# Top-k attention with a channel mix on one core: scaling the mix's differences on GpSimd, and one slot more between ranks and mask

## The chip, the core and the metric

The kernel runs on one core of a Trainium2 chip. Its engines are TensorE (PE in the rows; PEld its weight loads), VectorE (DVE), ScalarE (ACT), GpSimd (POOL) and SyncE (SP), which issues the DMAs. Each engine works through its own queue in order, and they wait for one another by semaphores. The metric is the time of one execution on the device in microseconds; lower is better.

## What is computed

Attention over 8 batches, 8 heads, 576 positions and head size 64, in which every query keeps its 32 largest scores alone, and behind it a channel mix with a shift by one token (512 channels, 1024 inside):

```python
scores = scale * np.matmul(q, k.transpose(0, 1, 3, 2))
kth = np.partition(scores, -top_k, axis=-1)[..., -top_k:-top_k + 1]
scores = np.where(scores >= kth, scores, -1e9)
attn = softmax(scores)                       # over the kept ones
x = (attn @ v) laid out as (B, S, H * D)
x_prev = x shifted by one token
xk = mu_k * x + (1.0 - mu_k) * x_prev        # xr the same with mu_r
k = np.maximum(xk @ w_k, 0.0)
out = sigmoid(xr @ w_r) * (k * k @ w_v)
```

All tensors are float32. Where a matrix product of the mix needs more precision than one pass has, values are split into a coarse and a remaining part and three products are summed.

## The kernel before

**Tiles.** A tile of attention is 128 rows by 576 keys: 128 queries of one head, or the last 64 queries of two heads. A pair of heads has nine tiles, a batch 36, all of it 288. The mix goes over 19 chunks of tokens, most of 256 (`SIZES`).

**Slots.** The function `pipeline` writes the order of work out by hand, under a manual schedule. Each turn of its main loop is a slot, in which every engine gets one step of each of several tiles: tile n begins, and the older tiles n-1, n-2 and so on (`A`, `C`, `M`, `V`, `W`) are at later steps. The string `ORDER` gives the order of the steps in a slot; as each engine takes its instructions in the order in which they are issued, `ORDER` sets the order in each queue. A tile goes through these slots:

- slot n: TensorE makes the scores (lines 192 and 197, PSUM tile `ps`), ScalarE copies them to `sc` (`keep`, line 202).
- slot n+1: VectorE takes the eight best of each of seven pieces of a row (`c0` to `c6`, line 226): 56 candidates.
- slot n+2: VectorE ranks the candidates, three rounds of eight (lines 229 and 232), and writes the two bounds into `seen` (lines 237 and 238). ScalarE then takes the sign of every score against the 24th best, and a sum of it (`count`, line 242, tile `sg`). GpSimd multiplies it by the scores (`below`, line 245), which leaves the scores beneath the bound to be told from the others.
- slot n+3: ScalarE writes the exponentials to PSUM (`exp`, line 253, tile `se`; the tile is n-`EXPS`). VectorE takes the eight best of the product (`eighth`, line 819), picks the threshold by the count (`thr`, line 250), and masks the exponentials (`mask`, line 256, tile `E`).
- slot n+4: TensorE turns the masked tile (line 269), ScalarE copies it out (line 273); for the last tile of a group, VectorE takes the reciprocals of the row sums (line 283) and GpSimd spreads them (line 288, tile `rb`).
- slot n+5: TensorE turns these (line 294) and weighs the values (line 321). Slot n+6: VectorE scales the outcome into `xT` (`place`, lines 327 and 329).

**The mix** is handed to the slots in pieces by a planner, the class `Lanes`. Pieces of TensorE work (lines 377 to 379) go into the step `mix`, at most four a slot, as far as a budget reaches. Work of ScalarE and GpSimd waits in a queue for each of them (`L.soft`), with a planned cost, and is issued in the step `act` or `pool`, near the end of the slot, once what it depends on has been issued and the engine's budget for the slot allows. The function `begin` prepares a chunk twice, for the gate and for the hidden layer, in two halves of the channels: `change` takes the differences of neighbouring tokens (GpSimd, line 348), `share` multiplies them by 1 - mu, one scale per partition (ScalarE, line 353), and `add` adds the token (GpSimd, line 358). `finish` splits the sum into coarse (ScalarE, line 372) and remaining part (GpSimd, line 373). Behind the hidden layer GpSimd also works on its squares (lines 397 and 398). At the start the weights are prepared in the same slots (lines 121 to 158). When the tokens of a chunk aren't there yet, the mix waits (`"later"`).

Of the kernel before, what the change touches and what calls it, by code (L numbers as in the profile page):

```python
# [9 lines left out]
F32 = mybir.dt.float32  # L10
# [3 lines left out]
AF = mybir.ActivationFunctionType  # L14
OP = mybir.AluOpType
PSUM = bass.MemoryType.PSUM

B, H, S, D = 8, 8, 576, 64
# [18 lines left out]
NEG = -3.0e38  # L37
PACE, TENSOR, SHARE, PIECE, CAP, MOST = 4.60, 3.90, 0.74, 0.71, 4.45, 4
END, HASTE = 36, 0.56
EXPS, EVAC = 3, (0, 'et')  # L40
ORDER = """exp wpool high wmul norm evac best0 c0 drop0 c1 best1 c2 drop1 first score turn inv loads keep sign c3 best2 c4 bounds eighth norm2 count et late below act c5 early thr c6 mask place mix weigh wpe dve pool weights""".split()


@with_exitstack
def topk_attention_channel_mix(ctx: ExitStack, tc: tile.TileContext, q, k, v, mu_k, mu_r, w_k, w_v, w_r, out):
    nc = tc.nc
# [17 lines left out]
    nmu = consts.tile([128, 2, HP], F32, name="nmu")  # L64
# [8 lines left out]
    def open_pools(stack, g, sfx):  # L73
        p = lambda n, bufs, **kw: stack.enter_context(tc.tile_pool(name=n + sfx, bufs=bufs, **kw))
        g.one = p("one", 1)
        g.two = p("two", 2)
        g.three = p("three", 3)
        g.four = p("four", 4)


        scored = p("psS", 1, space=PSUM).tile([128, 2, 512], F32, name="ps")
        g.ps = scored[:, :, :HS]
        g.sums = scored[:, :, HS:HS + 128], scored[:, 0, HS + 128:HS + 192]

        se = p("psE", 1, space=PSUM).tile([128, 2 * 512], F32, name="se")
        g.pe, g.ranks = se[:, :S], se[:, S:S + 9]
        nc.vector.tensor_copy(g.ranks, ranks_i)
        g.ready = range(3 * HP + NFB) if sfx else []
        g.psM = p("psM", 4, space=PSUM)
# [108 lines left out]
        return g.ps  # L198

    def keep(g, T):  # L200
        T.sc = g.four.tile([128, S], F32, name="sc")
        nc.scalar.activation(T.sc.rearrange("p (e k) -> p e k", e=2), T.ps, AF.Copy)  # L202

    def pick_exact(g, T):
        top = g.four.tile([128, TOPK], F32, name="top")
# [34 lines left out]
    def count(g, T):  # L240
        T.side = g.two.tile([128, S], F32, name="sg")
        nc.scalar.activation(T.side, T.sc, AF.Sign, bias=T.under, scale=-BELOW, accum_out=T.cnt)  # L242

    def below(T):
        nc.gpsimd.tensor_mul(T.side, T.sc, T.side)  # L245
# [87 lines left out]
    def begin(g, pieces, which, n, L):  # L333

        halves = [Env() for _ in range(2)]
        for i, X in enumerate(halves):
            parts = []
            for h in (0, 1):
                o = 0
                for xT, s, m in pieces:  # L340
                    parts.append((h, o, xT, s, m))
                    o += m

            def change(X=X, parts=parts, h0=2 * i):
                if which:
                    g.change[h0 // 2] = g.one.tile([128, 2, CH], F32, name=f"xd{h0}")
                for _, o, xT, s, m in parts[:len(pieces)]:
                    nc.gpsimd.tensor_sub(g.change[h0 // 2][:, :, o:o + m], xT[:, h0:h0 + 2, s:s + m], xT[:, h0:h0 + 2, s + 1:s + 1 + m])

            def share(X=X, h0=2 * i):  # L350
                X.xm = g.two.tile([128, 2, CH], F32, name="xm")
                for h in (0, 1):
                    nc.scalar.activation(X.xm[:, h, :n], g.change[h0 // 2][:, h, :n], AF.Copy, scale=nmu[:, which, h0 + h:h0 + h + 1])

            def add(X=X, parts=parts, h0=2 * i):
                for _, o, xT, s, m in parts[:len(pieces)]:
                    d = X.xm[:, :, o:o + m]
                    nc.gpsimd.tensor_add(d, d, xT[:, h0:h0 + 2, s + 1:s + 1 + m])

            l = g.shared[i]  # L360
            if which:
                l = [L.soft("pool", 0.0046 * n + 0.05 * len(pieces), change, *l)]
            g.shared[i] = [L.soft("act", 0.0021 * n + 0.12, share, *l)]
            X.mixed = L.soft("pool", 0.0046 * n + 0.05 * len(pieces), add, *g.shared[i])
        return halves

# [235 lines left out]
    def pipeline(g):  # L602
        L = Lanes()
# [17 lines left out]
        xT, tiles, state = {}, {}, {"tokens": 0, "wait": 0, "start": 0, "held": []}  # L621
# [75 lines left out]
        def coming(n):  # L697

            for p in range(1, len(visits)):
                t = n - starts[p]  # L700
                if -5 <= t <= 5:
                    yield Ps[p] if p in Ps else new_pair(p), t

        total = len(where)
# [2 lines left out]
        load_mu()  # L707
        units = {}
        n = 0
        while n < total + 7 or "next" in state or L.busy():  # L710
            p, i = where[n] if n < total else (None, None)
            A, C, M, V, W = (tiles.get(n - d) for d in (1, 2, 3, 4, 5))
            X = tiles.get(n - EXPS)
            last = W if W and ends(W) else None

            def loads():
                for N, t in coming(n):
                    early = N.n > 1
                    if N.own and t == (-5 if early else -4):
                        load_keys(g, N, N.batch, N.hp)  # L720
                    if t == (-4 if early else -3):
                        load_queries(g, N, N.batch, N.hp, N.c0, N.c1)
                    if t == 5:
                        load_v(g, N, N.batch, N.hp)
                L.run("dma")

# [66 lines left out]
                    bounds(g, C)  # L793

            def count_():
                if C:
                    count(g, C)
                    L.use("act", 0.76)

            def below_():  # L800
                if C:
                    below(C)
                    L.use("pool", 1.36)

            def keep_():
# [22 lines left out]
                    L.use("dve", 3.4)  # L828

            def place_():  # L830
                T = tiles.get(n - 6)
                if T and ends(T):
                    U = T.U
                    if U.P.b not in xT:
                        if state["start"] < (U.P.b - 1) * S:
                            save()
                        if U.P.b > 1:
                            L.force(g.read)
                        xT[U.P.b] = new_batch(g, U.P.b)
                    U.xT = xT[U.P.b]  # L840
                    place(U)
                    if U.P.last and T.i == U.P.part[-1]:
                        state["tokens"] = U.P.b * S + (S if T.i == 8 else 256)
                if V and V.i == V.P.part[-1] and V.P.last:
                    o = slice(V.P.first, V.i + 1)
                    nc.vector.tensor_reduce(least[:, V.P.n // HP:V.P.n // HP + 1], V.P.group[:, :, 1:, o], axis=mybir.AxisListType.XYZ, op=OP.min)

            do = dict(loads=loads, score=score, turn=turn_, inv=inv, exp=exp, weigh=weigh_, norm=norm, norm2=norm2, bounds=bounds_,
                      count=count_, below=below_, keep=keep_, mix=mix, eighth=eighth, thr=thr, mask=mask_, place=place_, weights=weights)
# [12 lines left out]
    with ExitStack() as stack:  # L862
        g = Env()
# [15 lines left out]
    with tc.If(again > 0):  # L879
        with tc.For_i(0, B, 1) as b, ExitStack() as stack:  # L880
            g = Env()
            open_pools(stack, g, "_again")
            L = Direct()
            xT = new_batch(g)
            rows = out[bass.ds(b, 1)].rearrange("o s d -> (o s) d")
            for hp in range(HP):
# [3 lines left out]
                for i in range(9):  # L890
                    T = Tile_()
# [52 lines left out]
```

## Time and profile before

| | |
|---|---|
| time, median of 3 runs | 1282.28 us (1280.83 to 1283.04) |
| the profiled execution's own time | 1280.38 us |
| its span, first to last instruction | 1278.5 us |
| TensorE busy | 1149.8 us |
| VectorE busy | 1107.6 us |
| ScalarE busy | 1043.6 us |
| GpSimd busy | 903.1 us |
| mean granted share of TensorE's clock | 0.952 |

The span is what the trace covers; the execution's own time has 1.9 us more around it, and it lies 1.9 us below the median of the runs. Busy times of groups of instructions can sum to more than their engine's, since neighbouring instructions overlap a little. The name in front of an arrow in a row is the tile that is written, those behind it are read; L245 is line 245 of the kernel before.

### The profile page before, as it was taken

The page shows a single profiled execution, that of the slowest core. Times are in us where ns is not written, and L with a number is a line of the kernel's source. Part 1 is how long each engine was busy: PE and PEld are TensorE (multiplying, and loading weights), DVE is VectorE, ACT ScalarE, POOL GpSimd, SP SyncE. Part 2 cuts the span into 40 slices and gives each one's busy share as a digit, 9 for nine tenths or more (in the row PEclk, how much of TensorE's full clock was granted, in tenths as well). Part 3 has the DMA queues.
Part 4 walks back from the last instruction along what each step waited for, and adds up shares of the span by engine and source line. Part 5 has one row for each costly group of instructions (what it writes and reads, how often), then busy time and mean ns, then how long its engine had stood idle before and what let it go on. Part 6 is the DMA issues. An engine that isn't in the chain of part 4 may idle for free.

```text
span 1278.5 us, 33370 instructions
## 1 busy us (share of the span) xinstructions
PE 1149.8 (90%) x10757; PEld 893.0 (70%) x10757; DVE 1107.6 (87%) x6368; ACT 1043.6 (82%) x2494; POOL 903.1 (71%) x829
## 2 busy tenths in 40 slices
PE   5767798996989898889989999999999998999997
PEld 2435586774868686676867677877787786778886
DVE  5999999999989899899999999999999998998000
ACT  4786988988888888798989889989899988898431
POOL 5998765757676766586668777778677857777652
PEclk8787899998989899799999999999999998999999
DMA  5332122112111122112211122122211221111000
GB/s 160 122 108 79 31 59 62 34 41 65 50 51 50 29 73 62 36 28 64 64 55 41 29 72 63 40 57 52 65 51 39 65 64 44 51 30 28 13 17 24
DMA packets 113768, 69.37 MB, mean 54 GB/s; under 512 B 81840, under 2 KB 106416, under 8 KB 113584
## 3 DMA queue, kind: packets, MB, share of 16 engines
q1 hardware_dynamic: 113584, 67.14, 19.1%
q8 instruction: 88, 1.44, 0.5%
q14 instruction: 96, 0.79, 0.2%
HBM read 57.68 MB, written 9.44 MB: 52 GB/s over the span
## 4 chain that ended last, share of the span: by engine, by line
PE 49%; DVE 22%; ACT 14%; POOL 11%; issue 2%; SPq 1%; DMA 0%; ACTq 0%; DVEq 0%; POOLq 0%
PE ps L321 10%; PE ps L192 7%; DVE cand L226 5%; DVE top L819 4%; POOL sg L245 4%; DVE E L256 4%; ACT sc L202 4%; PE pv L377 4%; PE pv L379 3%; PE pt L269 3%; PE ph L377 3%; PE pv L378 3%; PE ph L378 3%; PE ph L379 3%; ACT sg L242 3%; PE pz L377 2%
## 5 line engine op out<-in xcount | busy, mean ns | idle before, releaser
L245 POOL TENSOR_TENSOR sg<-sc,sg 128x576 f32<-128x576 f32 x288 | 409.5, 1422 | 251.9 <-ACT sg L242 251.2
L226 DVE MAX8 cand<-sc 128x8 f32<-128x82 f32 (+1 forms) x2016 | 466.8, 232 | 1.6 <-ACT sc L202 1.4
L202 ACT ACTIVATE sc<-ps 128x576 f32<-128x576 f32 x288 | 188.8, 656 | 120.7 <-PE ps L192 54.7
L819 DVE MAX8 top<-sg 128x8 f32<-128x576 f32 x288 | 217.2, 754 | 31.2 <-POOL sg L245 29.1
L242 ACT ACTIVATE sg<-sc,seen 128x576 f32<-128x576 f32 x288 | 224.3, 779 | 18.9 <-DVE seen L237 16.1
L256 DVE SCALAR_TENSOR_TENSOR E<-sc,seen,se 128x576 f32<-128x576 f32 x288 | 231.8, 805 | 0.8 <-DVE cand L226 0.6
L192 PE MATMUL ps<-K,qs 64*128 64x288 f32 x1024 | 202.6, 472 | 32.7 <-ACT sc L202 16.2
L253 ACT ACTIVATE se<-sc,seen 128x576 f32<-128x576 f32 x288 | 218.8, 760 | 12.0 <-DVE E L256 10.7
L273 ACT ACTIVATE et<-pt 128x320 f32<-128x320 f32 x576 | 219.4, 440 | 1.5 <-PE pt L269 0.8
L321 PE MATMUL ps<-et,v_in 128*64 128x128 f32 (+1 forms) x2560 | 177.0, 286 | 44.1 <-ACT sc L202 39.6
L321 PEld LDWEIGHTS ps<-et,v_in 128*64 128x64 f32 x2560 | 146.7, 149 | 69.7 <-ACT sc L202 56.1
L269 PEld LDWEIGHTS pt<-ident,E 64*128 64x128 f32 x2880 | 135.6, 142 | 76.4 <-issue 19.7
L377 PE MATMUL ph<-xh,wk 128*128 128x256 f32 (+2 forms) x608 | 178.4, 293 | 0.0
L229 DVE MAX8 top<-cand 128x8 f32<-128x56 f32 x864 | 176.7, 205 | 0.1
L378 PE MATMUL ph<-xl,wk 128*128 128x256 f32 (+2 forms) x608 | 170.9, 281 | 0.5 <-POOL xl L373 0.5
L379 PE MATMUL ph<-xh,wk 128*128 128x256 f32 (+2 forms) x608 | 169.8, 279 | 0.0
L269 PE MATMUL pt<-ident,E 64*128 64x64 f32 x2880 | 143.5, 227 | 14.1 <-DVE top L229 10.6
L192 PEld LDWEIGHTS ps<-K,qs 64*128 64x128 f32 x1024 | 81.2, 193 | 95.2 <-issue 23.0
L377 PE MATMUL pv<-wv,hh 128*128 128x512 f32 (+1 forms) x296 | 125.6, 424 | 0.0
L379 PE MATMUL pv<-wv,hl 128*128 128x512 f32 (+1 forms) x296 | 118.6, 401 | 5.6 <-POOL hl L398 5.6
L377 PEld LDWEIGHTS ph<-xh,wk 128*128 128x128 f32 x608 | 115.4, 190 | 5.1
L378 PE MATMUL pv<-wv,hh 128*128 128x512 f32 (+1 forms) x296 | 117.1, 396 | 0.0
(91 smaller groups left out, 2286.2 us busy)
## 6 DMA issues: line engine op xcount, KB each, us to landing
v_in<-in_v SPq DMA_DIRECT2D x128, 128.0 KB, 2.7
qs<-in_q SPq DMA_DIRECT2D x64, 160.0 KB, 3.0
K<-in_k SPq DMA_DIRECT2D x64, 144.0 KB, 2.9
out<-eb SPq DMA_DIRECT2D x35, 256.0 KB, 2.1
qs<-in_q SPq DMA_DIRECT2D x64, 128.0 KB, 2.7
hh<-in_moe_w_v SPq DMA_DIRECT2D x6, 512.0 KB, 3.3
hh<-in_moe_w_k SPq DMA_DIRECT2D x5, 512.0 KB, 4.2
vr_in<-in_v SPq DMA_DIRECT2D x64, 32.0 KB, 2.3
```

The costliest lines, as they stand in the source:

```text
L192: nc.tensor.matmul(g.ps[:, e], lhsT=P.qs[h, j, x:x + 128], rhs=P.K[h, j], start=True, stop=True)
L202: nc.scalar.activation(T.sc.rearrange("p (e k) -> p e k", e=2), T.ps, AF.Copy)
L226: nc.vector.max(T.cand[:, 8 * i:8 * i + 8], T.sc[:, CUTS[i]:CUTS[i + 1]])
L242: nc.scalar.activation(T.side, T.sc, AF.Sign, bias=T.under, scale=-BELOW, accum_out=T.cnt)
L245: nc.gpsimd.tensor_mul(T.side, T.sc, T.side)
L256: nc.vector.scalar_tensor_tensor(T.e, T.sc, T.thr, g.pe, op0=OP.is_ge, op1=OP.mult, accum_out=T.rs)
L269: nc.tensor.transpose(pt[:, c * 64:(c + 1) * 64], T.e[h, k0:k0 + 128], ident[h, h])
L321: nc.tensor.matmul(pa[hs[j]], lhsT=lhsT, rhs=ms[c][j], start=(c == 0), stop=(c == NKC))
L377: nc.tensor.matmul(ps, lhsT=sh, rhs=mh, start=first, stop=False)
L378: nc.tensor.matmul(ps, lhsT=sh, rhs=ml, start=False, stop=False)
L379: nc.tensor.matmul(ps, lhsT=sl, rhs=mh, start=False, stop=last)
L819: nc.vector.max(M.top[:, 24:32], M.side)
```

## The change

The multiplication in `share` goes from ScalarE to GpSimd, as a `tensor_scalar` with the scale of each partition, and into the planner's queue for GpSimd. Between the ranks and the mask of a tile lies one slot more: count and product are made in slot n+3, and they are the first steps of the slot in `ORDER`, the count ahead of the exponentials in ScalarE's queue and the product ahead of all else in GpSimd's. Exponentials, eighth best, threshold and mask come in slot n+4 (`EXPS` is 4), and all that follows comes a slot later too. The scores `sc` get five buffers instead of four, the values are loaded a slot later, and the loop runs for one slot more.

```diff
@@ -37,8 +37,8 @@
 NEG = -3.0e38
 PACE, TENSOR, SHARE, PIECE, CAP, MOST = 4.60, 3.90, 0.74, 0.71, 4.45, 4
 END, HASTE = 36, 0.56
-EXPS, EVAC = 3, (0, 'et')
-ORDER = """exp wpool high wmul norm evac best0 c0 drop0 c1 best1 c2 drop1 first score turn inv loads keep sign c3 best2 c4 bounds eighth norm2 count et late below act c5 early thr c6 mask place mix weigh wpe dve pool weights""".split()
+EXPS, EVAC = 4, (0, 'et')
+ORDER = """count below exp wpool high wmul norm evac best0 c0 drop0 c1 best1 c2 drop1 first score turn inv loads keep sign c3 best2 c4 bounds eighth norm2 et late act c5 early thr c6 mask place mix weigh wpe dve pool weights""".split()
 
 
 @with_exitstack
@@ -76,6 +76,7 @@
         g.two = p("two", 2)
         g.three = p("three", 3)
         g.four = p("four", 4)
+        g.five = p("five", 5)
 
 
         scored = p("psS", 1, space=PSUM).tile([128, 2, 512], F32, name="ps")
@@ -198,7 +199,7 @@
         return g.ps
 
     def keep(g, T):
-        T.sc = g.four.tile([128, S], F32, name="sc")
+        T.sc = g.five.tile([128, S], F32, name="sc")
         nc.scalar.activation(T.sc.rearrange("p (e k) -> p e k", e=2), T.ps, AF.Copy)
 
     def pick_exact(g, T):
@@ -350,7 +351,7 @@
             def share(X=X, h0=2 * i):
                 X.xm = g.two.tile([128, 2, CH], F32, name="xm")
                 for h in (0, 1):
-                    nc.scalar.activation(X.xm[:, h, :n], g.change[h0 // 2][:, h, :n], AF.Copy, scale=nmu[:, which, h0 + h:h0 + h + 1])
+                    nc.gpsimd.tensor_scalar(X.xm[:, h, :n], g.change[h0 // 2][:, h, :n], nmu[:, which, h0 + h:h0 + h + 1], 1.0, op0=OP.mult, op1=OP.mult)
 
             def add(X=X, parts=parts, h0=2 * i):
                 for _, o, xT, s, m in parts[:len(pieces)]:
@@ -360,7 +361,7 @@
             l = g.shared[i]
             if which:
                 l = [L.soft("pool", 0.0046 * n + 0.05 * len(pieces), change, *l)]
-            g.shared[i] = [L.soft("act", 0.0021 * n + 0.12, share, *l)]
+            g.shared[i] = [L.soft("pool", 0.0033 * n + 0.05, share, *l)]
             X.mixed = L.soft("pool", 0.0046 * n + 0.05 * len(pieces), add, *g.shared[i])
         return halves
 
@@ -698,7 +699,7 @@
 
             for p in range(1, len(visits)):
                 t = n - starts[p]
-                if -5 <= t <= 5:
+                if -5 <= t <= 6:
                     yield Ps[p] if p in Ps else new_pair(p), t
 
         total = len(where)
@@ -707,9 +708,9 @@
         load_mu()
         units = {}
         n = 0
-        while n < total + 7 or "next" in state or L.busy():
+        while n < total + 8 or "next" in state or L.busy():
             p, i = where[n] if n < total else (None, None)
-            A, C, M, V, W = (tiles.get(n - d) for d in (1, 2, 3, 4, 5))
+            A, C, B_, M, V, W = (tiles.get(n - d) for d in (1, 2, 3, 4, 5, 6))
             X = tiles.get(n - EXPS)
             last = W if W and ends(W) else None
 
@@ -720,7 +721,7 @@
                         load_keys(g, N, N.batch, N.hp)
                     if t == (-4 if early else -3):
                         load_queries(g, N, N.batch, N.hp, N.c0, N.c1)
-                    if t == 5:
+                    if t == 6:
                         load_v(g, N, N.batch, N.hp)
                 L.run("dma")
 
@@ -793,13 +794,13 @@
                     bounds(g, C)
 
             def count_():
-                if C:
-                    count(g, C)
+                if B_:
+                    count(g, B_)
                     L.use("act", 0.76)
 
             def below_():
-                if C:
-                    below(C)
+                if B_:
+                    below(B_)
                     L.use("pool", 1.36)
 
             def keep_():
@@ -828,7 +829,7 @@
                     L.use("dve", 3.4)
 
             def place_():
-                T = tiles.get(n - 6)
+                T = tiles.get(n - 7)
                 if T and ends(T):
                     U = T.U
                     if U.P.b not in xT:
```

## Rows read from the trace of the kernel before

**Rows 1.** The page, parts 1 and 2: whole span; busy tenths in forty slices.

```profile
PE 1149.8 (90%) x10757; PEld 893.0 (70%) x10757; DVE 1107.6 (87%) x6368; ACT 1043.6 (82%) x2494; POOL 903.1 (71%) x829
...
PE   5767798996989898889989999999999998999997
...
DVE  5999999999989899899999999999999998998000
```

**Rows 2.** Windows, from:to and length, busy us of each engine (instructions).

```profile
core 0: us, PE busy (x) PEld busy (x) DVE busy (x) ACT busy (x) POOL busy (x), PEclk, DMA share, GB/s
...
130.00:690.00 560.00, 501.04 (x4942) 394.91 (x4942) 524.91 (x3104) 483.27 (x1166) 382.02 (x351) 0.94 0.19 49
690.00:1045.00 355.00, 339.53 (x3431) 270.06 (x3430) 343.51 (x2034) 321.08 (x781) 264.99 (x243) 1.00 0.20 54
1045.00:1181.00 136.00, 130.53 (x1289) 104.84 (x1287) 124.75 (x722) 118.89 (x290) 99.76 (x90) 0.97 0.15 41
1181.00:1278.50 97.50, 88.94 (x587) 73.99 (x583) 6.90 (x16) 30.29 (x71) 48.17 (x55) 0.97 0.05 18
```

**Rows 3.** Waits of the whole span: us in total, times, longest.

```profile
DVE top L819 <- POOL sg L245: 29.1, 72, 0.8
...
ACT sg L242 <- DVE seen L237: 16.1, 22, 1.8
...
DVE rs L283 <- ACT rs L279: 8.0, 12, 1.9
...
DVE xT L327 <- ACT sc L202: 6.3, 7, 1.5
DVE nine L250 <- ACT se L253: 5.8, 12, 0.9
...
DVE cand L226 <- ACT sc L202: 1.4, 2, 1.1
```

**Rows 4.** Waits of VectorE from 130 to 690 us.

```profile
DVE top L819 <- POOL sg L245: 16.0, 40, 0.8
```

**Rows 5.** Timeline from 168 us: start, length, instruction, [idle before <-releaser].

```profile
168.30 0.76 PE L192 MATMUL ps<-K,qs 64*128 64x288 f32 x4
...
169.18 0.65 ACT L202 ACTIVATE sc<-ps 128x576 f32<-128x576 f32 x1 [1.23 <-issue]
...
169.72 0.77 ACT L242 ACTIVATE sg<-sc,seen 128x576 f32<-128x576 f32 x1
...
170.13 0.23 DVE L226 MAX8 cand<-sc 128x8 f32<-128x82 f32 x1
...
170.66 1.43 POOL L245 TENSOR_TENSOR sg<-sc,sg 128x576 f32<-128x576 f32 x1 [2.74 <-ACT sg L242]
...
172.12 0.76 DVE L819 MAX8 top<-sg 128x8 f32<-128x576 f32 x1 [0.46 <-POOL sg L245]
```

**Rows 6.** Timeline from 421 us.

```profile
421.32 0.40 POOL L288 TENSOR_SCALAR rb<-rs 128x256 f32<-128x256 f32 x1
...
421.69 1.40 POOL L245 TENSOR_TENSOR sg<-sc,sg 128x576 f32<-128x576 f32 x1
...
423.12 0.76 DVE L819 MAX8 top<-sg 128x8 f32<-128x576 f32 x1 [0.70 <-POOL sg L245]
```

**Rows 7.** Lines by shape: count | busy us, mean ns of one | idle before.

```profile
L353 ACT ACTIVATE xm<-xd,nmu 128x256 f32<-128x256 f32 x128 | 54.6, 512 | 0.1
...
L147 POOL TENSOR_SCALAR hl<-hl 128x512 f32<-128x512 f32 x20 | 38.3, 1916 | 11.3 <-ACT hl L146 11.3
...
L288 POOL TENSOR_SCALAR rb<-rs 128x256 f32<-128x256 f32 x64 | 25.9, 405 | 31.6 <-DVE cand L226 27.6 <-PE pt L269 2.1 <-DVE rs L283 1.9
...
L288 POOL TENSOR_SCALAR rb<-rs 128x128 f32<-128x128 f32 x32 | 9.5, 298 | 12.1 <-DVE cand L226 9.7 <-PE pt L294 2.4
```

**Rows 8.** Timeline of TensorE at the end: last attention matmuls, first gate matmul behind.

```profile
1190.23 0.29 PE L321 MATMUL ps<-et,vr_in 128*64 128x64 f32 x4
...
1218.36 0.39 PE L377 MATMUL pz<-wr,xh 128*128 128x512 f32 x1
```

## The prediction

> **What bounds the kernel now.** I read the page first. TensorE is busy for 1149.8 us of the 1278.5 us span and VectorE for 1107.6; in the forty slices VectorE stands at 8 or 9 from the second slice until it drops to 0 in the last three, where TensorE alone is at 9 [rows 1]. So there are two parts: the loop of 288 attention tiles, and a tail in which only TensorE's channel mix is left. The table of windows puts the border at 1181 us [rows 2]: behind it TensorE works for 88.9 of 97.5 us and VectorE for 6.9. In the loop the two are close. From 130 to 690 us VectorE is idle for 560 - 524.9 = 35.1 us and TensorE for 59.0. From 690 to 1045 us it is 11.5 against 15.5, and from 1045 to 1181 us 11.3 against 5.5. VectorE is the nearer bound for most of the loop, and TensorE at its end.
>
> Then the list of waits, to see what VectorE's idle time is made of [rows 3]. The largest is the eighth best score (line 819), which waits for GpSimd's product (line 245): 29.1 us in 72 waits, all of it after 130 us and half of VectorE's 57.9 us of idle there. 16.0 us of it lie before 690 us [rows 4], so 13.1 after. The next ones are several times smaller: the reciprocal 8.0, the output's scaling (line 327) 6.3, the threshold behind the exponential 5.8. VectorE waits for new scores (line 226 behind line 202) for only 1.4 us.
>
> I followed each wait of line 819 back to its cause, gaps down to 0.06 us included (89 gaps, 30.9 us). There are two kinds.
>
> Of the first kind are 51 gaps with 17.2 us: GpSimd itself was idle until the count came, and ScalarE counted late because in its queue the count stands behind the copy of the new scores, which was late itself, for TensorE or for long ScalarE work ahead. One stands for all [rows 5]: the scores begin on TensorE at 168.30, the copy at 169.18, the count at 169.72, the product at 170.66, and the eighth best at 172.12, 0.46 us late. The count's own inputs had long been there.
>
> Of the second kind are 38 gaps with 13.7 us: GpSimd had no idle time ahead of the product, which stood in its queue behind mix work and, in 34 of the 38, directly behind the spread of the reciprocals (line 288). In one of them the spread begins at 421.32, the product at 421.69, the eighth best at 423.12, 0.70 us late [rows 6].
>
> **The count first in ScalarE's slot.** The count moves into the next slot, ahead of the exponential. In the circular order of ScalarE it changes places only with the copies of the turned tiles and the mix work behind them. The order from one copy of scores to the next exponential holds the same work as before, so the exponential isn't delayed by it. The eighth best moves by a whole slot (288 slots end at 1181 us, 4.1 us in the mean). So the count no longer stands behind the copy of scores on its way to the eighth best. In the example the copy began at 169.18 after 1.23 us of idle ScalarE; copy, this idle time and the exponential ahead of it are what the count overtakes [rows 5]. The worst wait was 0.8 us [rows 3] and the copy alone lasts 0.65 [rows 5], so I take the first kind at 17.2 us before and 0 to 2 us after. The count's own wait for its bounds (16.1 us of ScalarE [rows 3]) goes too: the bounds are a slot old by then. Queued behind the count are now the exponential and the copy; its inputs come before the mask for which the exponential waits anyway, so this new order costs nothing while ScalarE keeps up. If ScalarE lags, the threshold pays, which today waits 5.8 us for the exponential.
>
> **The product first in GpSimd's slot.** It passes the spread, 0.405 us for 256 columns [rows 7], but not the mix work that the slot before left in the queue. Taking at most 0.35 us off each of the 34 gaps behind a spread removes 9.7 of the 13.7 us and leaves 4.0. Behind the product the spread now waits 1.4 us longer at most; it is used by TensorE a slot later, and I cost it at nothing. If that cover were gone, TensorE would stand 96 times (64 + 32 spreads) for up to 1.4 us.
>
> **The scaling of differences.** 152 instructions leave ScalarE (128 of 256 columns at 0.512 us [rows 7]) and come to GpSimd. Neither engine bounds the loop. GpSimd's price isn't in the trace for this form with a scale per partition. From below: the spread, also a GpSimd multiply of one tensor of 128x256 by constants, 0.405 us. From above: half of line 147's 1.916 us for 128x512, so 0.958; that one takes a maximum and is the slowest of its kind [rows 7]. I take 0.405, as the operation is the same multiply. That makes 152 x 0.405 = 62 us at most on an engine that is idle for 178 us between 130 and 690 us and 90 between 690 and 1045 [rows 2]. On average there is room. Locally there isn't always: each of 19 chunks has two runs of four such instructions, 1.62 us a run, in the queue ahead of a product. I let that give back 3 us of the second kind, from 0 to 10 us.
>
> A rule speaks against this part. On the chip's row the multiply is cheaper on GpSimd (0.405) than on ScalarE (0.512) [rows 7]. The Trainium skill, GPSIMD Engine Reference, section 4.1, advises VectorE for elementwise work, since GpSimd is about twice as slow on two tensors, though near line rate on one. By its factor of two on ScalarE's row, an estimate, GpSimd would get 156 us instead of 62; the sum here goes by the rows of this case.
>
> **One slot more.** All tokens come one slot later. At the end this is covered: the last attention matmul starts at 1190.23 us, but the first mix matmul that needs the last tokens only at 1218.36, and TensorE is full of older mix work in between [rows 8]. The last chain (count, product, eighth best, mask) isn't longer, only spread over more slots. At the start the mix begins one slot later, and TensorE has that much more of it left later: 0 (the added drain slot takes it) to 4.1 us. I take 2.
>
> **The sum.** Of 30.9 us, 17.2 + 13.7, about 1 + 4 + 3 = 8 stay, so 23 go. Not all of it reaches the end. In the example the next candidates (170.13) begin only 0.3 us after the copy of scores ends (169.83) [rows 5], so VectorE, 0.46 us earlier, would meet that wait instead; and after 1045 us TensorE has only 5.5 us of idle time to give. I count 0.8: 18 us. Less ScalarE work should shorten the reciprocal's and threshold's waits (13.8 us together) by 2. With 2 for the later start: 18 + 2 - 2 = 18 us. The profiled execution took 1280.4 us, span and 1.9 us around it; 1262.4 for it, and with the median 1.9 above that execution, **1264 us**.
>
> **The rivals.**
> First, the candidates take over: VectorE catches TensorE's scores, and what line 819 no longer waits comes back at line 226. For it: TensorE's small idle share after 690 us. Against it: line 226 waits 1.4 us today. With TensorE as the bound from 690 us on and half of the 16.0 us kept before: 8 - 2 = 6 us, 1276.
>
> Second, slower: the runs of scaling on GpSimd. Where a product already ends a run of GpSimd work, as in the second kind [rows 6], the 1.62 us ahead of it would go into VectorE's wait. 38 runs x 1.62 = 62 us is the whole price; with half of it, 31 us, against 13 us that remain of the gain and 2 for the start, 1282 + 31 - 13 + 2 = 1302. It decides the sign from about 18 / 38 = 0.5 us of each run on. With 0.958 us per instruction a run is 3.8 us, and it is passed sooner. Against it: GpSimd's idle time ahead of products, and line 245's many starts behind an idle engine.
>
> Third, it doesn't do what it says: the product still comes last, since the mix work of the slot before stays ahead of it and the later count eats the slot. Then 1282, within 0.2%.
>
> Fourth, more than said: the waits of the reciprocal, the output's scaling and the threshold also go, as VectorE and TensorE get more room. 20 us of idle time on top of it, nearly all passed on: 1245.
>
> **How the numbers follow.** Forecast 0.60 (its own range 1253 to 1273), candidates 0.15, GpSimd's runs 0.12, no effect 0.08, more 0.05. Below 1248 and above 1283 lie 0.04 and 0.13, so the range is 1248 to 1283. A measurement of this kernel tells about 0.2%, 2.6 us, from no change. Faster: 0.60 + 0.05 + 0.14 of the first rival = 0.79. Same: 0.08 + 0.01 = 0.09. Slower: 0.12.
>
> **What would show it.** In the changed kernel's waits, line 819 behind line 245 should be at 8 us or less, and the count's wait for the bounds gone. GpSimd's busy time should grow by some 60 us and ScalarE's fall by some 60, with single instructions of line 354 near 0.41 us. VectorE's busy time stays, its idle time between 130 us and its end falls from 58 to about 38, and the tail behind the loop keeps its 97 us within 4. If line 226 waits over 10 us, the first rival has it; if line 819 still waits with GpSimd busy ahead, the second or third. The forecast is wrong if the tail grows by what the loop loses, for instance because the mix falls behind in the loop.

## The result, and the profile after

The changed kernel takes 1251.0 us in the median (1250.75 to 1251.24) against 1282.6 of the kernel before: 0.9756 of it, with an interval from 0.9739 to 0.9773. It is faster by 31.6 us where 18 were forecast. The profiled execution took 1251.07 us with a span of 1249.2. All line numbers behind 78 are one higher in it than before.

The page first, its line of busy times and VectorE's forty slices; [rows 1] show the same of before.

```profile
PE 1144.4 (92%) x10757; PEld 889.2 (71%) x10757; DVE 1100.0 (88%) x6368; ACT 996.7 (80%) x2342; POOL 969.1 (78%) x981
...
DVE  4999999999999999999999999999999999997000
```

The kinds of work are the same, but ScalarE has 47 us less (1043.6 before) and GpSimd 66 us more (903.1). VectorE stands at 9 in almost every slice, where it was at 8 or 9.

The next two views are tables of windows, at borders that match in both kernels: from the end of tile 24's mask to the end of the last mask, and from there to the end. First before, then after; the columns are as in [rows 2].

```profile
154.30:1181.70 1027.40, 952.55 (x9484) 756.30 (x9481) 972.03 (x5730) 901.76 (x2183) 729.33 (x669) 0.97 0.19 50
1181.70:1278.50 96.80, 88.24 (x580) 73.46 (x578) 6.20 (x14) 29.81 (x70) 47.47 (x54) 0.97 0.05 18
```

```profile
156.60:1151.00 994.40, 943.67 (x9476) 750.35 (x9474) 963.04 (x5713) 863.28 (x2055) 782.39 (x792) 0.97 0.19 52
1151.00:1249.20 98.20, 89.43 (x588) 74.53 (x584) 6.21 (x14) 22.71 (x51) 55.69 (x74) 0.98 0.05 18
```

The loop lost 33.0 us (1027.4 to 994.4), the start before it took 2.3 us longer (154.3 to 156.6), and the tail 1.4. In the loop VectorE's idle time fell from 55.4 to 31.4 us, and its busy time by 9.0. A small part of that is 17 instructions fewer between these borders (5713 against 5730); over the whole span the number is the same, 6368, and the busy time fell by 7.6 us (1107.6 to 1100.0). TensorE's idle time fell as well, from 74.9 to 50.7 us.

The waits of the changed kernel, in total, times and longest, to be held against [rows 3]:

```profile
ACT se L254 <- DVE E L257: 18.3, 57, 0.6
ACT sg L243 <- DVE top L820: 16.5, 21, 2.6
...
DVE rs L284 <- ACT rs L280: 8.7, 15, 2.5
...
DVE nine L251 <- ACT se L254: 8.0, 14, 1.2
...
DVE xT L328 <- ACT sc L203: 6.1, 8, 1.5
...
DVE top L820 <- POOL sg L246: 3.8, 4, 1.4
```

VectorE's wait for the product (line 820) fell from 29.1 to 3.8 us and from 72 times to 4. Its waits for ScalarE stayed: reciprocal 8.7, threshold 8.0, the output's scaling 6.1. ScalarE's count no longer waits 16.1 us for its bounds but 16.5 for the eighth best: with two buffers for the product it has to wait until the one of two tiles before is read. Both waits lie almost wholly in the start: 2.6 us of the first and 1.7 us of the second fall into the loop.

The scaling itself, count, busy time and mean in ns:

```profile
L354 POOL TENSOR_SCALAR xm<-xd,nmu 128x256 f32<-128x256 f32 x128 | 59.9, 480 | 2.6
```

It takes 0.480 us for 256 columns on GpSimd, between the bounds of 0.405 and 0.958 [rows 7] and near the lower. A single one is a little shorter than ScalarE's 0.512, but neighbours overlap: ScalarE was busy for 54.6 us with its 128 [rows 7], 0.427 each, and GpSimd for 59.9, 0.468 each. So on GpSimd the work is about a tenth dearer.

### The profile page after: what moved, and what is told of

Same layout as the page of the kernel before. It is cut to its first block, busy times and chain, and to the rows that moved or that the text cites. A ratio compares the mean times of both kernels' runs of the same rounds, so it can differ in the third digit from the quotient of the medians.

```text
span 1249.2 us, 33255 instructions
## 1 busy us (share of the span) xinstructions
PE 1144.4 (92%) x10757; PEld 889.2 (71%) x10757; DVE 1100.0 (88%) x6368; ACT 996.7 (80%) x2342; POOL 969.1 (78%) x981
## 4 chain that ended last, share of the span: by engine, by line
PE 59%; DVE 21%; ACT 10%; POOL 7%; issue 1%; SPq 1%; DMA 0%; DVEq 0%; ACTq 0%; POOLq 0%
PE ps L322 11%; PE ps L193 9%; PE ph L378 5%; PE ph L379 5%; DVE cand L227 5%; PE ph L380 5%; DVE E L257 4%; PE pv L378 4%; PE pt L270 4%; PE pv L380 4%; PE pv L379 3%; ACT sc L203 3%; DVE top L820 3%; PE pz L378 2%; PE pz L379 2%; PE pz L380 2%
## 5 line engine op out<-in xcount | busy, mean ns | idle before, releaser
L243 ACT ACTIVATE sg<-sc,seen 128x576 f32<-128x576 f32 x288 | 227.9, 791 | 22.4 <-DVE top L820 16.5
L322 PE MATMUL ps<-et,v_in 128*64 128x128 f32 (+1 forms) x2560 | 171.9, 280 | 23.8 <-ACT sc L203 19.1
L322 PEld LDWEIGHTS ps<-et,v_in 128*64 128x64 f32 x2560 | 141.9, 145 | 48.4 <-ACT sc L203 35.7
L374 POOL TENSOR_TENSOR xl<-xm,xh 128x512 fp32r<-128x512 f32 (+2 forms) x76 | 91.8, 1226 | 47.5 <-ACT xh L373 47.5
L378 PE MATMUL pv<-wv,hh 128*128 128x512 f32 (+1 forms) x296 | 127.1, 430 | 0.0
```

Source lines behind the costliest of these rows:

```text
L322: nc.tensor.matmul(pa[hs[j]], lhsT=lhsT, rhs=ms[c][j], start=(c == 0), stop=(c == NKC))
L378: nc.tensor.matmul(ps, lhsT=sh, rhs=mh, start=first, stop=False)
```

## The experiments

Four waits of VectorE tell how late ScalarE is: the reciprocal for the row sums, the threshold for the exponential, the output's scaling and the candidates for the copy of scores. They are called its waits for ScalarE here; before they were 8.0 + 5.8 + 6.3 + 1.4 = 21.5 us [rows 3], in the changed kernel 22.8 (the candidates wait for nothing there). The wait for the product stands beside them. Each kernel was timed against the kernel before on its own chip. The table puts the first of them together, the others have their numbers in the text; "gain" is 1 minus the ratio.

| kernel | gain | wait for the product, us | waits for ScalarE, us |
|---|---|---|---|
| before | | 29.1 | 21.5 |
| scaling on GpSimd alone | 0.4% | 29.1 | 8.0 |
| added slot alone | -0.5% | 33.8 | 19.6 |
| added slot and new order | 0.6% | 0.9 | 45.4 |
| all three, product late | 2.0% | 5.7 | 21.5 |
| changed kernel | 2.4% | 3.8 | 22.8 |
| before, eighth best freed | 0.4% | 0 | 50.1 |
| the same, scaling on GpSimd | 0.8% | 0 | 36.1 |
| the same and added slot, old order | 0.8% | 0 | 36.8 |

**One part alone.** Scaling on GpSimd in the kernel before:

```diff
-nc.scalar.activation(X.xm[:, h, :n], ..., AF.Copy, scale=nmu[...])
+nc.gpsimd.tensor_scalar(X.xm[:, h, :n], ..., nmu[...], 1.0, op0=OP.mult, op1=OP.mult)
-g.shared[i] = [L.soft("act", 0.0021 * n + 0.12, share, *l)]
+g.shared[i] = [L.soft("pool", 0.0033 * n + 0.05, share, *l)]
```

> The kernel before with only the scaling moved to GpSimd; slots and order as before. Theory (the gain comes from the order and the added slot, and ScalarE doesn't bound): 1282 within 4 us, VectorE's wait for the product about 29 us as before, GpSimd busy up by some 70 us. Rival 1 (the relief of ScalarE carries a good part of the gain): 1270 or less. Rival 2 (GpSimd's runs delay the product): 1290 or more, with the wait for the product above 35 us.

It measured 1273.6 us against 1279.3, a ratio of 0.9959 (0.9944 to 0.9975). The gain is small, between theory and rival. The waits, VectorE's:

```profile
DVE top L819 <- POOL sg L245: 29.1, 61, 1.8
...
DVE xT L327 <- ACT sc L202: 3.1, 5, 0.8
DVE rs L283 <- ACT rs L279: 2.3, 7, 0.7
```

The product is waited for as before, while the waits for ScalarE fall from 21.5 to 8.0 us. GpSimd's runs do not delay the product in total (the longest single wait grew from 0.8 to 1.8 us), so the slower rival of the prediction has nothing here. The loop, between the same borders as above, is 11.1 us shorter than before (1016.3), but the tail is 4.0 longer (100.8) and the start 1.2.

The added slot alone, on the changed kernel with the scaling back on ScalarE and the old order:

```diff
-ORDER = """count below exp wpool ... eighth norm2 et late act ...
+ORDER = """exp wpool ... eighth norm2 count et late below act ...
```

> The changed kernel with the scaling back on ScalarE and count and product back at their old places within the slot, so that the added slot alone remains; the count takes a tile whose bounds are a slot old. Theory (the order frees the eighth best, not the slot by itself): 1282 within 4 us, wait for the product still 25 to 32 us, the count's wait for the bounds gone. Rival (a slot more between ranks and mask is what helps): 1262 or less.

1285.8 us, 1.0054 (1.0034 to 1.0073). As the theory had it, the slot by itself removes nothing; the wait for the product is even a little above the 25 to 32 us that it named:

```profile
DVE top L820 <- POOL sg L246: 33.8, 80, 2.1
```

and it costs 0.5%, some 7 us, which is more than the 2 us counted for the later start.

Slot and order, with only the scaling back on ScalarE (the first diff reversed, on the changed kernel):

> The changed kernel with only the scaling back on ScalarE. Theory: nearly the whole gain, 1250 to 1256, wait for the product under 6 us. Rival (the move of the scaling carries a third or more of it): 1261 or more.

1273.3 us, 0.9943 (0.992 to 0.9965). My theory fell here. The wait for the product is down to 0.9 us, but hardly any time is saved. The loop is 13.1 us shorter than before (1014.3), and the start takes 6.2 us of that back (160.5 against 154.3), for a reason that isn't traced. VectorE's waits for ScalarE are

```profile
DVE nine L251 <- ACT se L254: 19.5, 33, 1.6
...
DVE rs L284 <- ACT rs L280: 14.6, 26, 1.3
DVE xT L328 <- ACT sc L203: 10.9, 9, 2.3
```

45.0 us in these three rows, where they were 20.1 before. The timeline shows one of them, ScalarE's queue and the threshold:

```profile
522.26 1.73 ACT L354 ACTIVATE xm<-xd,nmu 128x256 f32<-128x256 f32 x4
...
523.85 0.80 ACT L243 ACTIVATE sg<-sc,seen 128x576 f32<-128x576 f32 x1
...
524.61 0.77 ACT L254 ACTIVATE se<-sc,seen 128x576 f32<-128x576 f32 x1
...
525.41 0.23 DVE L251 SCALAR_TENSOR_TENSOR nine<-se,cnt,top 128x9 f32<-128x9 f32 x1 [1.60 <-ACT se L254]
```

Four scalings stand together in ScalarE's queue, 1.73 us, right ahead of count and exponential, and the threshold starts 1.60 us late. In the loop of this run there are 31 such runs of four. VectorE's waits for ScalarE sum to 41.9 us there, against 19.3 in the changed kernel, and 12.3 of them come within 2 us of the end of a run, a stretch that makes up 11% of the loop. In the changed kernel 2.1 us come as close behind the scalings. So the runs of four explain about half of the difference directly; how their lag causes the rest is not traced.

**The price of the wait.** If this is so, taking away the wait for the product in the kernel before should give little, and more with the scaling moved. The eighth best reads the scores, so it never waits (these runs leave the product out of the threshold):

```diff
-nc.vector.max(M.top[:, 24:32], M.side)
+nc.vector.max(M.top[:, 24:32], M.sc)
```

> The kernel before in which the eighth best reads the scores themselves instead of GpSimd's product, so that VectorE never waits for the product; count and product are still made, but the threshold is then taken from wrong values, which this run leaves so. Theory (ScalarE's lag stands behind the wait for the product as the next bound, and the relief of ScalarE is needed to cash the gain): 1268 to 1276, and the waits for the exponential and the reciprocal, 14 us before, grow to 25 us or more. Rival (each microsecond of the wait for the product is worth one or more by itself, as the order alone was held back by something else): 1256 or less.

1276.0 us against 1281.1, 0.9962 (0.9948 to 0.9976), at the theory's upper end. The waits:

```profile
DVE rs L283 <- ACT rs L279: 19.1, 28, 2.2
DVE nine L250 <- ACT se L253: 18.4, 28, 1.6
...
DVE xT L327 <- ACT sc L202: 11.4, 9, 2.2
...
DVE cand L226 <- ACT sc L202: 1.2, 2, 1.0
```

29.1 us of waits for the product went, and the waits for ScalarE grew from 21.5 to 50.1, by 28.6, almost to the microsecond. VectorE's idle time in the loop is 55.3 us, as before (55.4). This profiled execution took 1281.7 us, 5.7 more than the median of this kernel's runs, so a typical one may have somewhat less of these waits.

The same with the scaling on GpSimd (the first diff and the one above, on the kernel before):

> The same with the scaling on GpSimd besides; still the order and the slots of the kernel before, and the same part of the threshold left wrong. Theory (the two causes only pay together, whatever the slots): 1247 to 1255, waits for the exponential and the reciprocal together under 15 us. Rival (the gain of the changed kernel needs its slot and order for more than the wait for the product): 1260 or more.

1272.0 us, 0.9925 (0.99 to 0.995). This was a miss: the two together are not enough. The waits for ScalarE fell only to 36.1 us:

```profile
DVE rs L283 <- ACT rs L279: 11.8, 23, 1.0
DVE xT L327 <- ACT sc L202: 9.8, 13, 2.3
DVE cand L226 <- ACT sc L202: 7.7, 9, 2.0
DVE nine L250 <- ACT se L253: 6.8, 13, 1.1
```

So a third thing in the changed kernel counts. Two differences on ScalarE were left: in the old place the count waits for its bounds, and it stands between the copy of scores and the copies of turned tiles. The next kernel has slot and scaling of the changed kernel and the freed eighth best, and only the old order besides, so that the count has its bounds from the slot before (the second diff and the one above, on the changed kernel):

> The changed kernel (added slot, scaling on GpSimd) with count and product back at their old places in the slot, and the eighth best freed of the product as before (it reads the scores, so the threshold is left wrong). VectorE then never waits for the product, the count never for its bounds, and only the count's place between the copy of scores and the copies of turned tiles differs from the changed kernel. Theory A (what the count cost in the middle of the slot was its wait for the bounds, 14 to 16 us of ScalarE): 1248 to 1256, VectorE's waits for ScalarE 25 us or less. Theory B (its place alone holds back what comes behind it): 1264 to 1274, waits for ScalarE 30 us or more.

1268.8 us against 1279.9, 0.9917 (0.99 to 0.9933): in the range of theory B. The waits:

```profile
DVE rs L284 <- ACT rs L280: 12.8, 19, 2.5
...
DVE xT L328 <- ACT sc L203: 11.6, 12, 2.3
...
DVE nine L251 <- ACT se L254: 7.9, 14, 1.2
...
DVE cand L227 <- ACT sc L203: 4.5, 5, 1.9
```

The waits for ScalarE stay at 36.8 us, 14 more than in the changed kernel, though the count waits for nothing. So the place in the slot matters by itself. The product went back along with the count; put back alone it costs some 4 us (the next run), against 18 here, which points to the count for most of it.

Why the place matters stays open. One reason would be that a count at the start of the slot runs in time in which ScalarE would wait for the mask anyway. The waits in the loop alone, of this run and then of the changed kernel, don't bear it out, since ScalarE waits for the mask about as long in both:

```profile
ACT se L254 <- DVE E L257: 11.3, 30, 0.9
...
POOL sg L246 <- ACT sg L243: 188.4, 107, 4.9
...
PE pv L380 <- POOL hl L399: 12.9, 7, 3.0
```

```profile
ACT se L254 <- DVE E L257: 12.8, 41, 0.6
...
POOL sg L246 <- ACT sg L243: 104.1, 77, 4.7
...
PE pv L380 <- POOL hl L399: 2.2, 3, 1.1
```

Two ways are left, and no run parts them: the count in the middle delays the copies of turned tiles behind it on ScalarE, or GpSimd, which stands 84 us longer for the count, comes later to the mix work behind the product, for which TensorE then waits 10.7 us more.

**Count and product apart.** The changed kernel with the product back behind the spread:

```diff
-ORDER = """count below exp ... et late act ...
+ORDER = """count exp ... et late below act ...
```

> The changed kernel with the product back behind the spread in GpSimd's queue, the count still first on ScalarE. Theory (the first kind of wait, 17 us, goes by the count's place, the second, 14 us, by the product's): some 10 us of the wait for the product come back, 1259 to 1264. Rival (the early count alone does it, since GpSimd starts its queue earlier): 1254 or less, wait under 6 us.

1255.0 us, 0.9804 (0.9785 to 0.9824), 0.5% more than the changed kernel, against the theory and close to the rival: of the 10 us that should come back, 2 did.

```profile
DVE top L820 <- POOL sg L246: 5.7, 9, 1.8
```

The early count does nearly all of it. The product still stands directly behind the spread for 94 tiles, as before, but GpSimd comes to both earlier. Its idle time ahead of the product, almost all of it for the count, first before and then in this run:

```profile
L245 POOL TENSOR_TENSOR sg<-sc,sg 128x576 f32<-128x576 f32 x288 | 409.5, 1422 | 251.9 <-ACT sg L242 251.2 <-PE ps L192 0.2
```

```profile
L246 POOL TENSOR_TENSOR sg<-sc,sg 128x576 f32<-128x576 f32 x288 | 408.2, 1423 | 54.6 <-ACT sg L243 53.9
```

Behind a spread the product ended 0.03 us before the eighth best in the median, and ends 0.67 us before it here.

**Without the scaling.** The changed kernel with the scaling left out on both engines (`add` reads the differences; the output lacks the factor):

```diff
-nc.gpsimd.tensor_scalar(X.xm[:, h, :n], g.change[h0 // 2][:, h, :n], nmu[...], 1.0, ...)
-nc.gpsimd.tensor_add(d, d, xT[...])
+nc.gpsimd.tensor_add(d, g.change[h0 // 2][:, :, o:o + m], xT[...])
```

> The changed kernel in which the scaling by 1 - mu is left out altogether, on both engines; the planner's order is unchanged. Theory (it is ScalarE's relief that counts, GpSimd's load costs next to nothing): 1247 to 1252, within 4 us of the changed kernel. Rival (the 70 us on GpSimd cost time that a cheaper place would save): 1245 or less.

1246.0 us against 1281.1, 0.9731 (0.9706 to 0.9755). The time lies between the theory's range and the rival's. Each held against its own kernel before, the two kernels differ by 0.25%, some 3 us, and their intervals overlap, so GpSimd's load costs from nothing to some 7 us. The waits for ScalarE are those of the changed kernel:

```profile
DVE rs L284 <- ACT rs L280: 8.2, 15, 2.5
DVE nine L251 <- ACT se L254: 7.6, 12, 1.2
...
DVE xT L328 <- ACT sc L203: 5.1, 6, 1.5
```

**Attempts at more.** The exponential ahead of the count, on the changed kernel:

```diff
-ORDER = """count below exp wpool ...
+ORDER = """exp count below wpool ...
```

> The changed kernel with the exponential ahead of the count in ScalarE's slot. Theory (what VectorE still waits for ScalarE, 8 us at the threshold, comes from the place of the exponential behind the count): that wait falls below 4 us, the wait for the product stays under 8 us, 1244 to 1251. Rival (the exponential then waits for the mask of the slot before and the count behind it, so the product is late again): 1254 or more with the wait for the product above 12 us.

1277.5 us against 1281.1, 0.997 (0.9957 to 0.9982). The theory's time and the rival's wait both fell: the threshold's wait is down to 1.7 us, the product's at 5.2, yet nearly all of the gain is lost. Of the 28 us between the two profiled executions, 17 are lost up to the mask of tile 18, while the weights are prepared (it ends at 151.0 us instead of 133.8). There it isn't a wait that grew, but one instruction of VectorE in the preparation of the weights, first here, then in the changed kernel:

```profile
L154 DVE TENSOR_SCALAR early<-early 128x512 uint32<-128x512 uint32 x20 | 28.9, 1447 | 0.7
```

```profile
L154 DVE TENSOR_SCALAR early<-early 128x512 uint32<-128x512 uint32 x20 | 8.8, 440 | 0.7
```

These 20.1 us more cover the loss in the start, where VectorE's idle time is no longer than in the changed kernel (22.1 and 25.0 us up to that mask). 17 of the 20 took 1.30 to 1.67 us, and each of these began just behind the start of a product on GpSimd, as here:

```profile
60.65 1.40 POOL L246 TENSOR_TENSOR sg<-sc,sg 128x576 f32<-128x576 f32 x1 [1.15 <-ACT sg L243]
...
60.67 1.66 DVE L154 TENSOR_SCALAR early<-early 128x512 uint32<-128x512 uint32 x1
```

The other three, with no GpSimd work beside them, took 0.43. The loop lost another 9.4 us (1003.8), and in it ScalarE waits 44.0 us for the mask instead of 12.8. The row of the whole span:

```profile
ACT se L254 <- DVE E L257: 85.2, 96, 4.2
```

With the exponential first, the count behind it cannot use this time.

The reciprocal later in VectorE's order, on the changed kernel:

```diff
-... eighth norm2 et late act c5 early thr c6 mask ...
+... eighth et late act c5 early thr c6 norm2 mask ...
```

> The changed kernel with VectorE's reciprocal (and the spread behind it) later in the slot, between the threshold and the mask. Theory (VectorE's wait for the row sums, 8.7 us, is one of the three waits for ScalarE that are left): it falls under 3 us and the time by 3 to 8 us, 1243 to 1248. Rival (the wait moves to the threshold, which now comes sooner behind the eighth best): that wait grows from 8 to 12 us or more, 1249 to 1253.

1249.7 us against 1279.9, 0.9766 (0.9749 to 0.9782): no difference from the changed kernel, as the rival had it. Of the 6.3 us that the reciprocal's wait lost, 3.7 came back at the threshold, which now waits 11.7.

```profile
DVE nine L251 <- ACT se L254: 11.7, 22, 1.5
...
DVE rs L284 <- ACT rs L280: 2.4, 1, 2.4
```

Then with the ranks in SBUF and three buffers for the product besides:

```diff
-g.pe, g.ranks = se[:, :S], se[:, S:S + 9]
+g.pe, g.ranks = se[:, :S], g.one.tile([128, 9], F32, name="ranks")
-T.side = g.two.tile([128, S], F32, name="sg")
+T.side = g.three.tile([128, S], F32, name="sg")
```

> The same with two more: the ranks stand in SBUF instead of the exponentials' PSUM tile, so that the threshold needn't wait for the exponential, and three buffers for the product instead of two, so that the count needn't wait for the eighth best of two tiles before (16.5 us of ScalarE). Theory (VectorE's idle time is what is left to take): VectorE's waits for ScalarE fall from 23 us to 10 or less, 1236 to 1244. Rival (TensorE bounds by now): the waits fall but the time doesn't, 1247 or more.

1298.1 us, 1.0135 (1.0113 to 1.0157): slower than the changed kernel and the one before. The waits for ScalarE fell to 6.7 us, but the threshold's instruction became long, 0.495 us in the mean instead of 0.223, 78.4 us more in all:

```profile
L251 DVE SCALAR_TENSOR_TENSOR nine<-ranks,cnt,top 128x9 f32<-128x9 f32 x288 | 142.6, 495 | 0.1
```

One of the long ones, with GpSimd's instruction beside it:

```profile
165.04 1.41 POOL L246 TENSOR_TENSOR sg<-sc,sg 128x576 f32<-128x576 f32 x1
165.06 1.42 DVE L251 SCALAR_TENSOR_TENSOR nine<-ranks,cnt,top 128x9 f32<-128x9 f32 x1
```

Last, with the ranks back in PSUM, three buffers, and the threshold directly ahead of the mask:

```diff
-... c5 early thr c6 norm2 mask ...
+... c5 early c6 norm2 thr mask ...
```

> The changed kernel with the reciprocal later, as in the run before, the threshold one piece of candidates later, directly ahead of the mask, and three buffers for the product; the ranks stay in PSUM. Theory (VectorE's waits for ScalarE are still worth their time): the wait for the exponential falls from 12 us to 7 or less, and the time to 1240 to 1247. Rival (TensorE and the start bound by now, or the waits move on): within 3 us of 1250.

1261.8 us against 1280.8, 0.9855 (0.9832 to 0.9879), slower than the changed kernel. The threshold's wait fell to 4.1 us, but the mask reads what the threshold has just written, and VectorE now stands idle before it for 20.8 us in 288 times (0.9 us in the changed kernel, where a piece of candidates lies between):

```profile
L257 DVE SCALAR_TENSOR_TENSOR E<-sc,seen,se 128x576 f32<-128x576 f32 x288 | 234.6, 815 | 20.8 <-PE ps L198 0.5 <-PE pt L295 0.5 <-PE pt L270 0.2
```

None of these beats the changed kernel by more than can be told.

## Why the prediction was right, and where its steps were off

**What bounds the loop** was right: VectorE, with TensorE close behind. The largest wait was the one that the change removed, and VectorE's time in the loop fell with it. The tail stayed within 1.4 us, as [rows 8] had it.

**The wait for the product.** Forecast 30.9 to 8 us of idle time before the eighth best, measured 4.1 us. The first kind of gap went by the early count, as said. For the second I gave the credit to the product's place ahead of the spread (9.7 us). The run with the product late shows 2 us of waits and 0.5% of time for it; the count's place does the rest, since an earlier count lets GpSimd empty its queue earlier. The prediction also miscounted: of the 38 gaps of the second kind 30, not 34, lie directly behind a spread, and 0.35 us off each at most makes 9.1 us instead of 9.7.

**The step that failed is how the parts add up.** I passed 0.8 of the removed wait on to the end, and gave the scaling's move 2 us. Slot and order alone give 0.6%, the scaling alone 0.4%, both together 2.4%; so the move, on top of slot and order, is worth 1.9%. Without it nothing like 0.8 passes: with slot and order alone 28.2 us of waits for the product go and 23.9 come back as waits for ScalarE (45.4 instead of 21.5), and with the eighth best freed 28.6 of 29.1 come back. With the move, 26.4 us of idle time before the eighth best in the loop went (30.5 to 4.1) and only 2.4 came back elsewhere. The sentence "Neither engine bounds the loop" rests on no row for ScalarE, and the view that I should have asked was the order of its queue: four scalings in a row there, 1.73 us, ahead of the exponential. These are shown as the cause of about half of what came back, and for the rest only that it goes with the move. The prediction named the threshold as the one that pays if ScalarE lags, but priced it at its wait of before (5.8 us), when VectorE was late anyway for the product and hid it.

**How much was luck.** The prediction had the wait and the direction right. The time lies outside the range that it gave the forecast itself (1253 to 1273) and 3 us inside the stated one. Too much was expected of slot and order (18 - 2 = 16 us; alone they gave 0.6%, some 7) and far too little of the scaling's move (2 us; 1.9% on top of them, some 24), and these two errors partly made up for each other.

**More than the idle time.** The loop lost 33.0 us, of which 24.0 are idle time. The other 9.0 are busy time of VectorE. Some 1.4 us of it are the 17 instructions that fall outside the borders; the rest is overlap. An eighth best that doesn't wait starts 0.06 us after the start of the bounds' last instruction (0.14 us long), and the two overlap; one that waits loses this overlap. Before, 99 of 263 in the loop started more than 0.1 us after it, in the changed kernel 9, and the lost overlap, at most 0.083 us each, sums to 8.2 and 0.7 us. So a wait costs its gap and the overlap, and gaps too short to be listed cost as well. The term of 18 us was mis-sized for this too; the prediction had it that VectorE's busy time stays.

**The scaling on GpSimd.** An instruction of 256 columns takes 0.480 us instead of 0.405, and the 152, some of them smaller, 69.4 us instead of 62, on an engine with room; the 3 us given back for its runs fit what the run without the scaling allows. GpSimd's busy time grew by 66.0 us where some 60 were expected, but ScalarE's fell by 46.9 and not by some 60. The second rival fell: the wait for the product is 29.1 us with the scaling alone, as before. The 156 us that the prediction estimated by the factor of two in the Trainium skill (GPSIMD Engine Reference, section 4.1) didn't come, and that section gives the factor for two inputs and against VectorE, and near line rate for one input. Measured against ScalarE's busy time the factor is 1.1 here (0.468 to 0.427 us); no run has this multiply on VectorE. The prediction's reading that it is cheaper on GpSimd set a single instruction's 0.405 against 0.512 and left out that ScalarE's overlap.

**The added slot.** 2 us forecast; the start took 2.3 us longer and the tail 1.4, and by itself the slot costs some 7 us (0.5%). The count's wait for its bounds went, but a wait for the eighth best came in its place, which the prediction didn't see: the scores got a fifth buffer, the product kept its two. In the loop both are small (2.6 and 1.7 us).

**The rivals.** The candidates didn't take over (VectorE waits for no new scores instead of 1.4 us). The third, that the product still comes last, fell with the wait of 3.8 us. The fourth, more than said, came nearest in time (1245), but for another reason: the other waits didn't go (22.8 us), the removed one was worth more.

## What to carry to other kernels

A wait that is removed is worth its time only if the next engine in line is on time; before adding up parts, ask of every wait behind the removed one what its releaser does in that slot, by its queue and not by its mean share. Two changes that give 0.4% and 0.6% alone can give 2.4% together, so a small result of one part is no reason to drop it. In an in-order queue, try the instruction whose inputs are oldest where the engine would wait anyway: with the exponential ahead of the count the loop was 9.4 us longer. And when an instruction becomes longer, look at what ran beside it on the other engines, before looking for waits.

## What the runs showed of the hardware

**Two inputs in SBUF.** A VectorE instruction over 9 columns took 0.22 us with one of its tensors in PSUM, and up to 1.45 us with both in SBUF. In the run with the ranks in SBUF 129 of 288 took over 0.3 us; each of these began while a GpSimd instruction was at work and ended within 0.04 us behind its end. In the changed kernel, with the ranks in PSUM, 213 of 288 began beside GpSimd and none took over 0.24 us. The Trainium skill (SBUF — State Buffer, "Who interferes with whom") says that a VectorE instruction with two SBUF inputs contends with a GpSimd instruction that reads SBUF. The 129 agree with it. 58 short ones also began beside GpSimd: 43 when it had at most 0.5 us left, and 15 beside line 148's instruction, 1.3 us before its end, which this sentence doesn't explain. The mask, with one input in SBUF and one in PSUM, keeps its 0.806 us in the changed kernel (0.805 before) though GpSimd works 66 us more.

**A `tensor_scalar` behind the start of a product.** In the run with the exponential first, VectorE's line 154 (512 columns of uint32) took 1.30 to 1.67 us instead of 0.43 in the 17 cases in which a GpSimd product had begun 0.02 to 0.4 us before it, and each of them ended 0.28 to 0.29 us behind that product.

**A result read at once.** In the run with the threshold directly ahead of the mask, which reads its result, VectorE stood idle before each mask, for 0.07 us in the mean (20.8 us in 288 masks). With one piece of candidates between them, as in the changed kernel, it is 0.9 us in all.
